# Block-sparse attention and a token/channel mixer: the queries of two more pairs of heads and the mask biases of two more pairs are turned by DMA, under a new order of the work

## Chip, cores and metric

The kernel runs on one core of one Trainium2 chip. The metric is the device time of one execution in microseconds; the time of a kernel is the median of its runs.

## The reference

Inputs are q, k and v, each [4, 8, 768, 64] (batch, head, position, width) in float32, and four weights. The core of the reference, with its shapes:

```python
k_rep = k.reshape(B, H, 12, 64, D).mean(axis=3)             # one mean key per block of 64
gate_scores = np.einsum('bhsd,bhnd->bhsn', q, k_rep)        # [B, H, 768, 12]
gate_scores = np.where(causal, gate_scores, -1e9)           # a query sees its own and earlier blocks
top_idx = np.argsort(gate_scores, axis=-1)[..., -3:]        # three best blocks, and the own block
...
mask = mask & (pos[:, None] >= pos[None, :])
scores = np.where(mask, scale * q @ k.T, -1e9)
attn_out = softmax(scores) @ v
...
x = attn_out.transpose(0, 2, 1, 3).reshape(4, 768, 512)
h = np.maximum(x.transpose(0, 2, 1) @ w_tok1, 0) @ w_tok2   # token mixing, 768 -> 256 -> 768
u = x + h.transpose(0, 2, 1)
h2 = np.maximum(u @ w_ch1, 0) @ w_ch2                       # channel mixing, 512 -> 1536 -> 512
out = u + h2
```

The three best blocks must be chosen as the reference chooses them, so the gate is computed from queries and key sums that are each held as the sum of two float16 numbers, a high part and a remainder.

## The kernel before

The 32 heads are worked on as 16 pairs, i = 0 to 15 (two heads of one batch side by side on 128 partitions). Four pairs make a batch, and when its attention is there, its mixer follows; pairs of the next batches run in between. A pair goes through these steps:

- **Loads** on the SP queue: `load_qk` (L379) brings ql (queries) and kl (keys) as two halves of 192 KB, `load_v` (L402) v.
- **Keys** are turned by six float32 transposes on TensorE (`transposes`, L436, tile tkl), evacuated from PSUM to kt (L482 ACT, L484 DVE), cast into KA, the operand of the scores (L806 on POOL, two casts per pair), and summed by block on DVE (`ksum`, L666, tile kst). POOL splits the sums in three small instructions (`split_sum`, L611 to L613; tiles ksums, kp).
- **Queries** are turned in one of two ways. For pairs below QTURN: six float32 transposes on TensorE (L436, tile tql), an evacuation to the high part qh (`evac_q`, L482 or L484) and one DVE instruction for the remainder qr, read from PSUM (`rest_q`, L520). From QTURN on: ACT scales and rounds ql to the high part (`split_hi`, L568, tile qn), DVE computes the remainder in SBUF (`split_rest`, L574), and two DMA transposes on the SP queue turn the two (`turn_q`, L579, to qh and qr). In both ways qh is copied into Q, the operand of the scores (`place_q`, two copies on POOL or ACT).
- **Gate**: ten matmuls qh, qr by kp (`gate_parts`, L644, tile gps), two additions on DVE (L656, L658), ten MAX8 (`top`, L675), a comparison (`below`, L685) and the mask bias bn (`bias`, L704), a float16 tile of 0 and -60000 per query and block.
- **Mask bias** turned in one of two ways. Below MTURN: five float16 transposes on TensorE (`mask`, L714, tile bps) and two copies into Q on DVE or ACT (`put_mask`, L804, L806). From MTURN on: one DMA transpose on the SP queue (`turn_m`, L693, tile mt) and two copies into Q on POOL or ACT (`place_m`).
- **Scores** (L736, tile sps), exponentials on ACT (L750, tile e), the diagonal's causal mask on DVE (L756) or POOL, attention times v (L772, tile aps), reciprocal and normalisation on DVE (L780, L791, tile x16).

The mixer of a batch: token products (L815, L827), u and its transpose uT by DMA (L421); the first channel product c = uT by wc1 (`ch1`, L896) with a relu on ACT (L798) or DVE (L800) to h2a and h2b; the second by seven block products (`prod`, L947) that need sums of h2 (s1, s3, s4) and four differences of the blocks of wc2: t3, t1, t2, t4 (`weight_sum`, L915, on DVE). The first three differences are taken once, before the first batch's second product; t3 is the first of them, and it reads all of the last half of wc2. The weights are loaded on POOL's queue: w for the tokens, wc1 in four loads (L1082), wc2 in four loads (L1084).

All this is written as a list of operations. `plan` (L225) puts them in the order of ORDER (L103) and sets from OTHER which operations run on their other engine, from LARGE which PSUM tiles take the larger kind, and from PLACES which copy of its buffer a tile takes. Each engine and each queue works in that order. A DMA transpose or a load is issued by SP when its turn comes, and SP waits at its head for the data that it reads or the buffer that it writes. So an operation's place in the list decides what waits behind it.

```python
QTURN = 10
MTURN = 9
...
            if t32 == "ql" and i >= QTURN:
...
            if i >= MTURN:
```

The first condition (L1117) chooses the way of the queries, the second (L1276) that of the mask bias.

## Time and profile before

| what | value |
|---|---|
| runs | 239.66, 238.57, 239.58 us |
| median | 239.58 us |
| profiled execution | span 237.6 us (the page gives the span alone) |
| instructions in the profile | 6633 |
| PE busy | 230.9 us, 97%, granted clock 0.9 or more of full speed in all 40 slices |
| DVE, ACT, POOL busy | 197.8, 158.5, 122.0 us |
| transfers | 35.60 MB, mean 150 GB/s |

The span runs from the profile's first instruction to its last. The median of the runs stands 1.98 us above it. Busy time is the time in which an engine had an instruction in work; PE is TensorE's matmuls, DVE VectorE, ACT ScalarE, POOL GpSimd, and SP the engine that issues most transfers. Idle time of an engine is put down to what ended it (its releaser).

### The profile page before, as it was taken

The numbers are of one execution on the slowest core, as the hardware profiler recorded it, in microseconds if no ns is written. First come the engines' busy times: TensorE is split into PE (matmuls) and PEld (weight loads), VectorE is DVE, ScalarE is ACT, GpSimd is POOL, SyncE is SP. The second block draws the span as 40 slices with busy tenths as digits, with TensorE's granted clock in tenths as the row PEclk, the third lists the DMA queues.
The fourth block names the chain that finished last, engine by engine and source line by source line (L and its number), as shares of the span: only waits on it lengthen the run. The fifth ranks groups of instructions, "written<-read, shape, count | busy, mean of one in ns | idle before, by whom it ended". The sixth has DMA issues, their size and how long they took to land.

```text
span 237.6 us, 6633 instructions
## 1 busy us (share of the span) xinstructions
PE 230.9 (97%) x2541; PEld 176.2 (74%) x2541; DVE 197.8 (83%) x604; ACT 158.5 (67%) x247; POOL 122.0 (51%) x214
## 2 busy tenths in 40 slices
PE   8899999999999999998999999999999999999994
PEld 6788889867777986784659885785768768666882
DVE  7999989999989999999799989995767678704861
ACT  6899998879879797869479675864778411064010
POOL 6899999258731364399530767354032132900560
PEclk9999999999999999999999999999999999999999
DMA  6999999999999698996936994973013015330033
GB/s 202 289 235 195 225 217 191 207 234 186 202 211 223 124 160 182 227 212 136 192 108 145 192 104 122 196 162 72 3 29 135 0 47 132 90 135 0 0 134 135
DMA packets 100208, 35.60 MB, mean 150 GB/s; under 512 B 90832, under 2 KB 96720, under 8 KB 100176
## 3 DMA queue, kind: packets, MB, share of 16 engines
q1 hardware_dynamic: 96400, 30.84, 58.7%
q0 software_dynamic: 3232, 3.93, 10.0%
q8 instruction: 20, 0.33, 0.6%
q10 hardware_dynamic: 544, 0.39, 0.5%
q14 instruction: 12, 0.10, 0.1%
HBM read 26.74 MB, written 6.29 MB: 139 GB/s over the span
## 4 chain that ended last, share of the span: by engine, by line
PE 84%; POOL 5%; DVE 4%; DMA 4%; ACT 1%; issue 1%; SPq 0%; ACTq 0%; DVEq 0%
PE c L896 24%; PE c L947 20%; PE sps L736 13%; PE aps L772 7%; PE ups L827 3%; PE tok L815 3%; DMA kl<-in_k_dram 2%; PE c L1003 2%; PE tkl L436 2%; POOL KA L806 2%; PE gps L644 1%; DMA mt<-bn 1%; POOL e L762 1%; PE tkl L449 1%; PE ups L860 1%; DVE qn L574 1%
## 5 line engine op out<-in xcount | busy, mean ns | idle before, releaser
L750 ACT ACTIVATE e<-sps 128x896 f16<-128x896 f32 (+2 forms) x96 | 84.7, 917 | 21.4 <-PE sps L736 20.8
L896 PE MATMUL c<-uT,wc 128*128 128x256 f16 (+1 forms) x384 | 69.4, 326 | 1.2 <-DVE h2a L800 1.2
L896 PEld LDWEIGHTS <-wc 128*128 128x128 f16 x384 | 36.3, 98 | 22.3 <-issue 1.7
L736 PE MATMUL sps<-Q,KA 128*128 128x128 f16 (+7 forms) x384 | 50.8, 259 | 0.3 <-ACT e L750 0.2
L969 POOL TENSOR_TENSOR vu<-v,u 128x256 f32<-128x256 f32 x33 | 24.9, 768 | 36.4 <-DVE v L962 35.0
L736 PEld LDWEIGHTS <-KA 128*128 128x128 f16 (+1 forms) x384 | 29.6, 97 | 13.9 <-issue 0.7
L806 POOL CAST KA<-kt 64x768 f16<-64x768 f32 x22 | 18.4, 836 | 19.9 <-ACT kt L482 18.1
L772 PE MATMUL aps<-V,e 128*128 128x65 f16 x672 | 25.6, 193 | 0.0
L772 PEld LDWEIGHTS <-e 128*128 128x128 f16 x672 | 24.2, 97 | 1.2
L798 ACT ACTIVATE h2a<-c 128x256 f16<-128x256 f32 (+1 forms) x27 | 13.0, 485 | 16.8 <-PE c L896 16.7
L947 PEld LDWEIGHTS <-s 128*128 128x128 f16 x198 | 18.9, 98 | 3.9
L800 DVE TENSOR_SCALAR h2b<-c 128x256 f16<-128x256 f32 (+1 forms) x24 | 13.2, 553 | 8.0 <-PE c L896 7.9
L791 DVE TENSOR_TENSOR x<-aps,rc 128x384 f16<-128x384 f32 x32 | 17.6, 551 | 0.4
L806 POOL COPY Q<-mt 12x320 f32<-12x320 f32 x10 | 4.9, 493 | 25.4 <-DMA mt<-bn 25.2
L947 PE MATMUL c<-t,s 128*128 128x256 f16 x132 | 17.7, 272 | 0.0
L756 DVE TENSOR_TENSOR e<-e,m 128x768 f16<-128x768 f16 x24 | 15.9, 668 | 1.9 <-ACT e L750 1.8
L800 DVE TENSOR_SCALAR h2a<-c 128x512 f16<-128x512 f32 (+1 forms) x21 | 11.5, 558 | 7.0 <-PE c L896 6.9
L798 ACT ACTIVATE h2b<-c 128x512 f16<-128x512 f32 (+1 forms) x24 | 11.5, 493 | 5.5 <-PE c L896 5.2
L947 PEld LDWEIGHTS <-h2a 128*128 128x128 f16 x132 | 12.5, 98 | 2.1 <-DVE h2a L932 0.2
L675 DVE MAX8 m<-gps 128x8 f32<-128x12 f32 x160 | 13.9, 160 | 0.2
L947 PEld LDWEIGHTS <-h2b 128*128 128x128 f16 x132 | 12.7, 98 | 1.8
L987 POOL TENSOR_TENSOR pc<-pc,pd 128x256 f32<-128x256 f32 x11 | 9.0, 817 | 8.6 <-ACT pc L804 6.5
(157 smaller groups left out, 456.7 us busy)
## 6 DMA issues: line engine op xcount, KB each, us to landing
v<-in_v_dram SPq DMA_DIRECT2D x16, 384.0 KB, 4.6
out_dram<-ob SPq DMA_DIRECT2D x23, 256.0 KB, 2.3
kl<-in_k_dram SPq DMA_DIRECT2D x28, 192.0 KB, 4.5
ql<-in_q_dram SPq DMA_DIRECT2D x26, 192.0 KB, 4.2
wc<-in_moe_w_ch_dram POOLq DMA_DIRECT2D x8, 384.0 KB, 8.4
kl<-in_k_dram SPq DMA_DIRECT2D x2, 384.0 KB, 5.7
ql<-in_q_dram SPq DMA_DIRECT2D x2, 384.0 KB, 7.1
w<-in_moe_w_tok_dram POOLq DMA_DIRECT2D x2, 384.0 KB, 7.9
```

The lines of the kernel that those rows point to most:

```text
L675: nc.vector.max(out=t[:, j, x, :], in_=T["gmx", i, m][:, j, x, :])
L736: nc.tensor.matmul(out=p[:, off + a:off + a + n], lhsT=KA[i % R][x][0:rows, 128 * kk:128 * kk + 128], rhs=QA[i % R][x][0:rows, q0 + a:q0 + ...
L750: nc.scalar.activation(out=e[:, 0:width], in_=T["sps", i, x, g][:, 0:width], func=AF.Exp, scale=scale)
L756: nc.vector.tensor_tensor(out=d, in0=d, in1=m0.broadcast_to([128, NJ, 128]), op=ALU.mult)
L772: nc.tensor.matmul(out=p[:, jq, :], lhsT=T["e", i, x, g][:, o:o + 128], rhs=V16[i % (R + 1)][:, x, kk, 0:65], start=(kk == 0), stop=(kk == ...
L791: nc.vector.tensor_tensor(out=T["x16", b][:, :, 64 * hh:64 * hh + 64], in0=T["aps", i, x][:, :, 0:64], in1=T["rc", i, x].broadcast_to([128 ...
L798: e.activation(out=out, in_=src, func=AF.Relu)
L800: e.tensor_scalar(out=out, in0=src, scalar1=0.0, scalar2=None, op0=ALU.max)
L806: e.tensor_copy(out=out, in_=src)
L896: nc.tensor.matmul(out=p, lhsT=wc1_16[:, cc, 128 * fc:128 * fc + 128], rhs=T["uT", b][:, a // 128:e // 128, cc, :], start=(cc == 0), stop= ...
L947: nc.tensor.matmul(out=T["c2" + key, b, j], lhsT=x[:, fc, :], rhs=y[:, fc, :], start=first and fc == 0, stop=fc == HF - 1, skip_group_chec ...
L969: nc.gpsimd.tensor_tensor(out=t, in0=T["v", b, j], in1=T["u", b][:, j + 3 * row, 256 * col:256 * col + 256], op=ALU.add)
```

## The change

Two numbers are changed: QTURN from 10 to 8 and MTURN from 9 to 7. So the queries of pairs 8 and 9 and the mask biases of pairs 7 and 8 take the way through the DMA transposes that the later pairs already took. No function is changed; each is three lines higher in the changed kernel, as ORDER is three lines shorter.

ORDER, OTHER, LARGE and PLACES are new throughout: every operation of the program may stand at another place, and the numbers of the operations are others, as some operations exist no more and others are new.

```diff
-QTURN = 10
+QTURN = 8
...
-MTURN = 9
+MTURN = 7
...
 ORDER = [
-    1471, 1479, 136, 137, 122, 123, 185, 184, 1459, 1468, 1483, 1465, 1476, 1464, 236, 1461, 1472, 1463, 1474, 1473,
...
+    288, 1475, 1463, 122, 2, 1472, 1478, 1477, 1461, 1482, 1465, 1486, 1464, 1466, 123, 137, 185, 3, 236, 0, 1474, 136,
...
```

What this makes of the engines' work: TensorE has 12 float32 transposes and 10 mask transposes fewer; SP issues 9 transposes of mask biases (7 before), 8 of qh and 8 of qr (6 and 6); DVE has 7 rows of work fewer and ACT 7 more, since some relus move from DVE to ACT; POOL has as many as before.

**SP, around the loads of the queries of pair 9** (a name's first number is the pair: kl_12 are the keys of pair 12; v32 is v). Before:

```order
L379 DMA kl_12_1436<-in_k_dram 128x6x64 x2
L379 DMA kl_9_1464<-in_k_dram 128x6x64 x2
L379 DMA ql_9_1562<-in_q_dram 128x6x64 x2
L379 DMA kl_10_1755<-in_k_dram 128x6x64 x2
L402 DMA v32_7_1811<-in_v_dram 128x12x64
L379 DMA ql_10_1838<-in_q_dram 128x6x64 x2
L402 DMA v32_8_1869<-in_v_dram 128x12x64
L379 DMA ql_11_1890<-in_q_dram 128x6x64 x2
```

After:

```order
L399 DMA v32_5_1504<-in_v_dram 128x12x64
L376 DMA kl_8_1518<-in_k_dram 128x6x64 x2
L576 DMA_TRANSPOSE qh_8_1527<-qn_8_1493 128x6x128
L576 DMA_TRANSPOSE qr_8_1600<-qn_8_1493 128x5x128
L399 DMA v32_6_1602<-in_v_dram 128x12x64
L690 DMA_TRANSPOSE mt_7_1673<-bn1_86 128x5x128
L376 DMA ql_9_1678<-in_q_dram 128x6x64 x2
L376 DMA kl_9_1842<-in_k_dram 128x6x64 x2
L376 DMA kl_10_1926<-in_k_dram 128x6x64 x2
L399 DMA v32_7_1931<-in_v_dram 128x12x64
```

Before, loads follow one another. Now the two transposes of pair 8's queries and the one of pair 7's mask bias (bn1) stand between the loads of keys 8 and queries 9, and the loads of keys 12, queries 10 and 11 stand later.

**POOL, around the split of pair 8's key sums** (KA and Q are operands of the scores, wc2 the weights of the second channel product; the first two of its four loads stand three rows ahead of the first piece). Before:

```order
L611 TENSOR_TENSOR ksums1_80<-kst_7_1458,heads_81 128x24
L612 CAST kp1_84<-ksums1_80 128x2x12
L613 TENSOR_TENSOR kp1_84<-ksums1_80,kp1_84 128x2x12
L1084 DMA wc2_90<-in_moe_w_ch2_dram 128x3x512
L806 COPY Q31_75<-qh_7_1352 64x384
L1084 DMA wc2_90<-in_moe_w_ch2_dram 128x3x512
L806 CAST V1_64<-v32_6_1376 128x12x64
L806 CAST KA_76<-kt_8_1637 64x768
L806 COPY Q30_74<-qh_7_1352 64x384
L611 TENSOR_TENSOR ksums0_79<-kst_8_1656,heads_81 128x24
L612 CAST kp0_83<-ksums0_79 128x2x12
L613 TENSOR_TENSOR kp0_83<-ksums0_79,kp0_83 128x2x12
```

After, where two earlier loads of wc2 stand ahead of the piece:

```order
L803 CAST V0_63<-v32_5_1504 128x12x64
L803 CAST KA_76<-kt_7_1323 64x768
L1081 DMA wc2_90<-in_moe_w_ch2_dram 128x3x512
L803 CAST KA_76<-kt_8_1630 64x768
L608 TENSOR_TENSOR ksums0_79<-kst_8_1676,heads_81 128x24
L609 CAST kp0_83<-ksums0_79 128x2x12
L610 TENSOR_TENSOR kp0_83<-ksums0_79,kp0_83 128x2x12
L803 COPY Q30_74<-qh_7_1362 64x384
L803 CAST KA_76<-kt_8_1630 64x768
L1081 DMA wc2_90<-in_moe_w_ch2_dram 128x3x512
L803 COPY Q31_75<-mt_7_1673 12x320
L803 COPY Q00_68<-qh_8_1527 64x384
```

Before, all four loads of wc2 stand ahead of pair 8's sums (ksums0 from kst_8). Now the third stands just ahead of them, and the fourth behind them, one copy of queries and one cast of keys. Pair 7's mask is copied by POOL from mt behind that load.

**DVE, from pair 8's gate to the first weight differences** (t3 and t1; gps is the gate, bn0 the mask bias of pair 8, e0 exponentials before the diagonal's mask). Before, where the first of the two copies of mask 7 stands two rows ahead of the piece, and pair 8's key sums and remainder three and two ahead of that copy:

```order
L806 COPY Q31_75<-bps_1709 12x640
L791 TENSOR_TENSOR x16_1_1444<-aps_1658,rc_1729 128x6x64
L756 TENSOR_TENSOR e0_6_1_1715<-e0_6_1_1715,m0_102 128x768
L800 TENSOR_SCALAR h2b_0_1335<-c1_1723 128x256
L656 TENSOR_TENSOR gm_8_1765<-gps_1736,gbias_100 128x120
L658 TENSOR_TENSOR gps_1736<-gps_1736,gm_8_1765 128x10x12
L675 MAX m8_8_1798<-gps_1736 128x8 x10
L685 TENSOR_TENSOR gps_1736<-gps_1736,m8_8_1798 128x10x12
L930 TENSOR_TENSOR s3_0_0_1825<-h2a_0_1330 128x768
L800 TENSOR_SCALAR h2a_0_1330<-c1_1760 128x256
L780 RECIPROCAL rc_1835<-aps_1776 128x6
L915 TENSOR_TENSOR t3_93<-wc2_90 128x1536
```

After, with pair 8's key sums eight rows ahead of the piece:

```order
L927 TENSOR_TENSOR s3_0_0_1768<-h2a_0_1325 128x768
L682 TENSOR_TENSOR gps_1716<-gps_1716,m8_8_1742 128x10x12
L701 SCALAR_TENSOR_TENSOR bn0_85<-gps_1716,own_101 128x10x12
L797 TENSOR_SCALAR h2b_0_1332<-c1_1730 128x512
L753 TENSOR_TENSOR e0_7_1_1773<-e0_7_1_1773,m0_102 128x768
L777 RECIPROCAL rc_1828<-aps_1775 128x6
L571 SCALAR_TENSOR_TENSOR qn_9_1797<-ql_9_1678,qn_9_1797 128x640
L753 TENSOR_TENSOR e0_6_1_1714<-e0_6_1_1714,m0_102 128x768
L788 TENSOR_TENSOR x16_1_1462<-aps_1775,rc_1828 128x6x64
L912 TENSOR_TENSOR t3_93<-wc2_90 128x1536
L753 TENSOR_TENSOR e0_7_0_1837<-e0_7_0_1837,m0_102 128x768
L912 TENSOR_TENSOR t1_91<-wc2_90 128x1536
```

Before, t3 stands behind the reciprocal that follows the gate's comparison. Now the mask bias, a relu, two diagonal masks, a normalisation and the remainder of pair 9's queries (qn_9) stand between the comparison and t3, and the copies of mask 7 are gone from DVE.

## Rows read from the trace of the kernel before

**Rows 1.** The page's part 1: busy us, share of the span, instructions
```profile
PE 230.9 (97%) x2541; PEld 176.2 (74%) x2541; DVE 197.8 (83%) x604; ACT 158.5 (67%) x247; POOL 122.0 (51%) x214
```

**Rows 2.** The page's part 4: the chain that ended last, by engine
```profile
PE 84%; POOL 5%; DVE 4%; DMA 4%; ACT 1%; issue 1%; SPq 0%; ACTq 0%; DVEq 0%
```

**Rows 3.** Two windows: us, PE, PEld, DVE, ACT, POOL busy, clock, DMA share, GB/s
```profile
48.00:60.00 12.00, 11.84 (x129) 8.21 (x128) 11.73 (x32) 9.82 (x18) 8.27 (x15) 1.00 1.02 204
60.00:72.00 12.00, 12.00 (x166) 9.23 (x164) 10.90 (x42) 9.52 (x15) 6.06 (x11) 1.00 1.19 207
```

**Rows 4.** The chain of waits, 79 to 84: start us, us, what
```profile
81.13 0.69 PE tql L436 x6
81.82 0.28 PE bps L714 x5
```

**Rows 5.** Groups by line and form: busy us, mean ns, idle before
```profile
L714 PE MATMUL bps<-id,bn 128*128 128x128 f16 x45 | 4.2, 219 | 0.2 <-DVE bn L704 0.2
L436 PE MATMUL tql<-id,ql 128*128 128x128 f32 x12 | 1.7, 277 | 0.0
```

**Rows 6.** Tiles qn and qr: ns min/median/max, first and last start us, forms
```profile
L568 ACT ACTIVATE qn<-ql x6: 827/839/846, 85.0 to 149.3; 128x768 f16<-128x768 f32 x6
L574 DVE SCALAR_TENSOR_TENSOR qn<-ql,qn x6: 810/816/2239, 89.9 to 150.8; 128x640 f16<-128x640 f32 x6
...
L520 DVE SCALAR_TENSOR_TENSOR qr<-tql,qh x2: 825/825/825, 66.5 to 82.8; 128x640 f16<-128x640 f32 x2
```

**Rows 7.** Timelines of DVE, POOL and PE, 108 to 114: start us, us, what
```profile
108.62 2.24 DVE L574 SCALAR_TENSOR_TENSOR qn<-ql,qn 128x640 f16<-128x640 f32 x1
...
108.90 0.50 POOL L806 COPY Q<-qh 64x384 f32<-64x384 f32 x1
...
112.45 1.89 PE L896 MATMUL c<-uT,wc 128*128 128x512 f16 x8 [1.07 <-DVE h2a L800]
```

**Rows 8.** Tile mt: instructions as in rows 6; landing us min/median/max
```profile
L806 POOL COPY Q<-mt x10: 441/446/717, 91.5 to 177.8; 12x320 f32<-12x320 f32 x10
L693 SPq DMA_TRANSPOSE mt<-bn x7: 1202/1211/1857, 88.1 to 173.3; - x7
...
DMA to landing us min/median/max: 2.6/2.8/4.2
```

**Rows 9.** Tile wc: landing of the weight loads, us
```profile
DMA to landing us min/median/max: 6.9/8.4/10.3
```

**Rows 10.** Timeline of POOL, 58 to 62: start us, us, what
```profile
58.04 0.50 POOL L806 COPY Q<-qh 64x384 f32<-64x384 f32 x1
...
60.20 0.80 POOL L1084 DMA_DIRECT2D wc<-in_moe_w_ch_dram  x1
...
61.51 0.78 POOL L1084 DMA_DIRECT2D wc<-in_moe_w_ch_dram  x1
```

**Rows 11.** Timeline of DVE, 65 to 74
```profile
65.01 0.95 DVE L666 TENSOR_REDUCE kst<-kt 128x12 f32<-128x768 f32 x1
...
69.24 0.54 DVE L791 TENSOR_TENSOR x<-aps,rc 128x384 f16<-128x384 f32 x1
69.70 0.54 DVE L756 TENSOR_TENSOR e<-e,m 128x768 f16<-128x768 f16 x1
...
73.13 0.92 DVE L915 TENSOR_TENSOR t<-wc 128x1536 f16<-128x1536 f16 x1
```

**Rows 12.** DMA issues, 49 to 52 and 57 to 59: KB each, median us to landing
```profile
ql<-in_q_dram SPq DMA_DIRECT2D x2, 192.0 KB, 4.4
kl<-in_k_dram SPq DMA_DIRECT2D x2, 192.0 KB, 4.2
...
wc<-in_moe_w_ch_dram POOLq DMA_DIRECT2D x2, 384.0 KB, 7.8
ql<-in_q_dram SPq DMA_DIRECT2D x2, 192.0 KB, 13.5
kl<-in_k_dram SPq DMA_DIRECT2D x1, 192.0 KB, 8.9
```

219 rows, old and new, of tables (LARGE, ORDER, OTHER, PLACES) are left out of this document.

## The prediction

> **What bounds the kernel now.** I read the busy line first: TensorE (PE) is busy for 230.9 of 237.6 us, VectorE (DVE) for 197.8, ScalarE (ACT) and GpSimd (POOL) for less [rows 1]. A busy share can hide waits, so the chain that ended last comes next: 84% of it is PE work, 4% DMA, 5% POOL, 4% DVE [rows 2]. So PE's own work sets the end, and a microsecond taken off PE is a microsecond won, unless another engine or a transfer then comes late. The stretch that the change works in is 48 to 72 us. There PE has next to no idle time at the full clock, DVE is busy for 11.73 and 10.90 of 12 us, and the DMA engines are full (1.02 and 1.19, overlapping packets counted twice) [rows 3]. DVE and the transfers are therefore next in line, and what is put on them there has little cover.
>
> The profiled execution has a span of 237.6 us; the page gives no time for what lies around it. The median of the three runs shown, 239.58, is 1.98 above the span. I add every term to the median, which supposes that these 1.98 us stay. A difference under 0.5%, 1.2 us, is what a measurement of this kernel can't tell from no change.
>
> **What leaves PE.** Two pairs lose six float32 transposes each, and two pairs lose five mask transposes each. In the chain, six float32 transposes take 0.69 us and five mask transposes 0.28 us [rows 4]. That is 2 x 0.69 + 2 x 0.28 = 1.9 us, and all of it lies on PE, with no wait before or behind. **Term 1: -1.9 us.** The rows of single transposes read 277 and 219 ns [rows 5]; these are latencies that overlap, since six of 277 would be 1.66 us and not 0.69. The Trainium skill ("TensorE: Matmul & The Clock Gate", Part 4: PE-mode transpose) gives about 275 ns per transpose in one kernel's context, which is the latency of the rows; as a price it would make the gain larger, and that is a rival below.
>
> **What other engines get.** Pairs 8 and 9 exchange one evacuation on ACT for one scaled split on ACT, and one remainder on DVE (0.825 us from PSUM) for one remainder on DVE (median 0.816, worst 2.239) [rows 6]. These cost the same, unless the remainder collides. One did: at 108.62 us it took 2.24 us while POOL worked without a break; the diagonal mask and the relu behind it on DVE were late by as much, and PE stood for 1.07 us at 112.45 [rows 6, 7]. It is the largest stall of PE after the start. In the new order another instruction may meet POOL there, or none. One of six remainders collided, and there will be eight, so one such stall somewhere is likely; but its cost hangs on what stands behind it. The ends are 0 and 1.1 us of gain, and I take the middle. **Term 2: -0.6 us** (-1.1 to 0).
>
> The mask copies of pairs 7 and 8 move from DVE and ACT to POOL and ACT, which wait for the transposes instead. POOL had room there, so I cost them at nothing. If POOL gave no cover, two copies of 0.45 us would be late by 0.9 us at pair 7; that end is in the range.
>
> **What the queues get.** SP issues six transposes more: the two of pair 8 and the mask of pair 7 now stand between the loads of k 8 and q 9 (first pair of order rows). Such a transpose lands 2.6 to 4.2 us after its issue, median 2.8 [rows 8]. Pair 7's mask bias is two DVE instructions ahead of pair 8's k sums, so the mask lands some 3 us after it and POOL copies it 0.5 us later; PE has over six other groups of matmuls up to pair 7's first scores. I cost this wait at nothing, and up to 1.4 us if it lands after 4.2.
>
> The Trainium skill ("VectorE: DVE Perf Modes", The three transpose paths and Rules for kernel authors) speaks against the change: it advises TensorE for a 128x128 transpose where PSUM will do, and gives 1309 ns for one by DMA against 390 on TensorE. By it five tiles would take 6.5 us, an estimate; the rows have 2.8 for the five, so here the measurement decides. By the page the mask of pair 7 would be about 1 us late, and the result within 0.5%.
>
> The weights are the edit that I think decides. All four wc2 loads stood before the k sums of pair 8 on POOL; now the last one stands behind them and behind two copies (second pair of order rows). Before, the last load was issued at 61.51 and DVE began the first weight difference, which needs all four, at 73.13: 11.6 us for a landing of 6.9 to 10.3 us, median 8.4 [rows 9, 10, 11]. Now count from the end of pair 8's k sums on DVE:
> - POOL does the copy of q, the cast of k, three small instructions for the sums, and then issues the load. The same five took from 58.04 to 60.20 us: 2.2 us [rows 10]. With a landing of 7.8 us (the two issued first, with little else of their queue in flight [rows 12]) the weights are there after 10.0 us; with 6.9 or 10.3, after 9.1 or 12.5.
> - DVE took from 65.96 (65.01 + 0.95) to 73.13 for what stood between, 7.2 us [rows 11]. Now one diagonal mask and one normalisation stand there more, and two mask copies less (third pair of order rows): about 7.5 us.
> - So DVE stands for 2.5 us (1.6 to 5.0). Behind it wait the diagonal mask of pair 7, the second difference and PE's first product that reads it. That product comes 9.3 us of matmuls after pair 8's gate (in the new order, at the chain's pace), and DVE needs 7.6 us plus the latency of 0.3 from the same gate to the end of the second difference. So 1.4 us are covered. **Term 3: +1.1 us** (0.2 to 3.6).
>
> **Sum:** -1.9 - 0.6 + 1.1 = -1.4 us, so 239.6 - 1.4 = **238.2 us**. Its own range goes from -1.9 - 1.1 + 0.2 = -2.8 (236.8) to -1.9 - 0 + 2.0 (239.7).
>
> **Rivals.**
> 1. *No change that can be told.* The weights land as late as the median and the collision comes back. Then term 3 is 2.2 - 1.4 - 7.5 + 8.4 = 1.7, up to 3.0 with the mask's wait (1.3 of the 1.4), and term 2 is 0: -1.9 + 1.7 to 3.0, about 239.9. For it: the stretch is full of transfers already [rows 3]. Against it: loads of k 12, k 14, q 10 and q 11 that stood here are issued later now.
> 2. *Slower: the load of q 9 lands late.* It stands directly behind the mask's transpose on SP, which waits for pair 7's bias. That bias leaves DVE 1.4 us before the k sums end; 1.2 us of issue for the transpose and two issues put the second half of q 9 at 1.0 us after the k sums. ACT splits it (0.84) and DVE's remainder of pair 9, three instructions ahead of the weight difference, waits for that. Up to a landing of 6.4 us it hides behind the weights (10.0 - 1.0 - 0.84 - 1.75 for the three). Loads of half a pair landed in 4.2 and 4.4 us with no weights in flight, but in 8.9 and 13.5 us when issued beside them [rows 12]. With 10.5 us the weight difference starts at 14.1 us instead of 7.5; less the 1.4 covered, PE loses 5.2, and ACT's exponentials queue behind the same split. So -1.9 - 0.6 + 5.2 = +2.7, **242.3 us**. It decides from a landing of 9.0 us on (+1.2 us). Against it: those slow ones had four weight loads and four halves of k around them; here the queue holds one load of v and one transpose just ahead, and one or two weight loads beside.
> 3. *Each transpose costs its latency.* 12 x 0.277 + 10 x 0.219 = 5.5 us off PE: 239.6 - 5.5 - 0.6 + 1.1 = 234.6. The chain speaks against it: six in 0.69 us [rows 4]. It is what the skill's figure in Part 4 would give.
>
> **How the numbers follow.** The forecast gets 0.55: 0.42 for below 238.4 and 0.13 for above. Rival 1 gets 0.20, rival 2 0.20, rival 3 0.03, and 0.02 is left for a new order that also removes the small stalls of the start. Faster by over 0.5%: 0.42 + 0.03 + 0.02 = 0.47. Within 0.5%: 0.13 + 0.20 = 0.33. Slower by over 0.5%: 0.20. The range leaves out rival 3 and the upper part of rival 2, some 0.16 together: 236.4 to 241.8 us, with 0.4 below the forecast's own end for the remainder.
>
> **What would show it.** Right: PE's busy time falls by about 1.9 us and its largest stall lies near 72 to 78 us, before a product that reads a weight difference, with DVE idle just ahead of the first difference on wc2; transposes of pairs 8 and 9 and of masks 7 and 8 landing in 2.6 to 5 us; no PE idle before the scores of pair 7. Term 3 is wrong if DVE has no idle time ahead of the first difference. Rival 2 shows as ACT idle on q before a split near 70 to 76 us, with that load landing after 9 us or more. The whole argument is wrong if PE's busy time doesn't fall, or if the new stalls lie outside 60 to 80 us, where I have priced nothing but the old one at 112 us.

## The result, and the profile after

| | median of the runs | profiled span |
|---|---|---|
| before | 239.57 us (238.57 to 239.66) | 237.6 us |
| after | 241.70 us (241.50 to 242.57) | 240.0 us |

The ratio of after to before is 1.0102, with a 95% interval of 1.0064 to 1.0140: the change makes the kernel slower by 2.4 us (1.5 to 3.4). All results below are such ratios against runs of the kernel before on the same chip, with the disturbed runs left out, so a difference of medians can differ from what the ratio gives. In microseconds a ratio is taken times 239.5.

Busy times of the profile after (they answer to [rows 1]) and, below them, its chain of waits by engine ([rows 2]):

```profile
PE 230.2 (96%) x2519; PEld 173.8 (72%) x2519; DVE 197.0 (82%) x597; ACT 162.6 (68%) x254; POOL 122.1 (51%) x214
```

The chain's shares:

```profile
PE 69%; POOL 9%; DVE 7%; DMA 5%; ACT 4%; issue 3%; SPq 2%; POOLq 0%; ACTq 0%; DVEq 0%
```

The 22 transposes are gone from PE (2541 matmuls before, 2519 now). Its busy time fell by only 0.7 us, though, and its idle time rose from 237.6 - 230.9 = 6.7 to 240.0 - 230.2 = 9.8 us. PE's share of the chain fell from 84% to 69%; what took its place is the other engines, DMA and SP's queue.

Windows of the profile after, columns as in [rows 3]:

```profile
60.00:72.00 12.00, 11.95 (x157) 8.74 (x156) 10.22 (x43) 11.86 (x20) 7.34 (x13) 1.00 1.17 179
72.00:84.00 12.00, 11.29 (x121) 9.13 (x120) 11.01 (x20) 11.11 (x20) 1.86 (x5) 1.00 1.05 176
84.00:96.00 12.00, 10.19 (x116) 7.20 (x113) 9.97 (x31) 8.71 (x14) 5.81 (x9) 1.00 1.14 207
108.00:120.00 12.00, 11.79 (x90) 7.11 (x87) 10.42 (x21) 10.06 (x16) 9.37 (x16) 1.00 1.07 194
```

From 72 to 96 us PE idles for 0.71 + 1.81 = 2.52 us. Before, it idled for nothing there. The DMA engines stay full up to 96 us and beyond, and DVE and ACT, which looked like the next bounds, have idle time as well: they wait too. In 108 to 120 us PE idles for 0.21 us, where the old stall of 1.07 us was.

Where the new idle time begins is seen in the chain of waits of the profile after, 68 to 91 us (start us, us, what):

```profile
68.59 3.64 DMA ql<-in_q_dram
...
83.74 4.96 DMA ql<-in_q_dram
...
88.80 0.85 ACT qn L565
...
89.68 0.83 DVE qn L571
```

and in the timelines of the profile after (start us, us, instruction, the wait before it and who ended it), first of ACT:

```profile
73.05 0.84 ACT L565 ACTIVATE qn<-ql 128x768 f16<-128x768 f32 x1 [0.81 <-DVE h2b L797]
...
88.80 0.84 ACT L565 ACTIVATE qn<-ql 128x768 f16<-128x768 f32 x1 [1.52 <-DMA ql<-in_q_dram]
```

of PE:

```profile
74.85 0.59 PE L733 MATMUL sps<-Q,KA 76*128 76x512 f16 x3 [0.71 <-ACT e L747]
...
90.39 0.59 PE L733 MATMUL sps<-Q,KA 128*128 128x512 f16 x3 [1.12 <-ACT e L747]
...
94.02 0.83 PE L944 MATMUL c<-t,h2a 128*128 128x256 f16 x6 [0.70 <-DVE h2a L929]
```

and of DVE:

```profile
76.01 0.96 DVE L912 TENSOR_TENSOR t<-wc 128x1536 f16<-128x1536 f16 x1 [0.33 <-issue]
```

The same thing happens twice. The load of queries 9, and then that of queries 10, is the last thing to come. ACT stands before the split of these queries; its exponentials queue behind the split, and PE stands before scores whose PSUM tile ACT has not read. At 73.05 the wait is put down to a DVE relu, which ended at 72.72 and which the split doesn't read; the chain goes back to the load. Its second half was issued at 68.55 and is listed as landed after 4.3 us, at 72.9, just before the split (its last transfer ended at 72.23 in the chain). At 88.80 DVE's remainder waits for the split in turn, and that makes the third stall of 0.70 us. The first weight difference, which the prediction feared for, waits for 0.33 us and stops nobody.

### The profile page after: what moved, and what is told of

Read it like the earlier page. It is cut to its first block, busy times and chain, and to the rows that moved or that the text cites. A ratio compares the mean times of both kernels' runs of the same rounds, so it can differ in the third digit from the quotient of the medians.

```text
span 240.0 us, 6634 instructions
## 1 busy us (share of the span) xinstructions
PE 230.2 (96%) x2519; PEld 173.8 (72%) x2519; DVE 197.0 (82%) x597; ACT 162.6 (68%) x254; POOL 122.1 (51%) x214
## 4 chain that ended last, share of the span: by engine, by line
PE 69%; POOL 9%; DVE 7%; DMA 5%; ACT 4%; issue 3%; SPq 2%; POOLq 0%; ACTq 0%; DVEq 0%
PE c L893 24%; PE c L944 15%; PE sps L733 9%; PE aps L769 6%; DMA ql<-in_q_dram 4%; POOL KA L803 3%; PE c L1000 2%; PE ups L824 2%; PE tok L812 2%; ACT e L747 2%; POOL Q L803 2%; PE warm L1019 2%; DMA out_dram<-ob 1%; POOL e L759 1%; PE ups L857 1%
## 5 line engine op out<-in xcount | busy, mean ns | idle before, releaser
L747 ACT ACTIVATE e<-sps 128x768 f16<-128x768 f32 (+2 forms) x96 | 85.5, 924 | 18.1 <-PE sps L733 12.9
L893 PE MATMUL c<-uT,wc 128*128 128x512 f16 (+1 forms) x384 | 70.0, 326 | 0.2 <-DVE rc L777 0.2
L733 PEld LDWEIGHTS <-KA 76*128 76x128 f16 (+1 forms) x384 | 29.9, 97 | 16.3 <-issue 3.2
L795 ACT ACTIVATE h2a<-c 128x512 f16<-128x512 f32 (+1 forms) x30 | 15.0, 500 | 12.4 <-PE c L893 12.1
L803 POOL CAST KA<-kt 64x768 f16<-64x768 f32 x22 | 19.4, 882 | 2.9 <-ACT kt L479 2.3
L797 DVE TENSOR_SCALAR h2b<-c 128x512 f16<-128x512 f32 (+1 forms) x22 | 12.4, 566 | 7.0 <-PE c L893 7.0
L795 ACT ACTIVATE h2b<-c 128x256 f16<-128x256 f32 (+1 forms) x26 | 12.4, 485 | 7.6 <-PE c L893 7.6
L753 DVE TENSOR_TENSOR e<-e,m 128x768 f16<-128x768 f16 x24 | 15.3, 643 | 1.1 <-ACT e L747 1.1
L803 POOL COPY Q<-mt 12x320 f32<-12x320 f32 x13 | 6.6, 507 | 15.9 <-DMA mt<-bn 15.5
L797 DVE TENSOR_SCALAR h2a<-c 128x256 f16<-128x256 f32 (+1 forms) x18 | 9.6, 539 | 4.8 <-PE c L893 4.6
```

What stands on the lines that cost most here:

```text
L733: nc.tensor.matmul(out=p[:, off + a:off + a + n], lhsT=KA[i % R][x][0:rows, 128 * kk:128 * kk + 128], rhs=QA[i % R][x][0:rows, q0 + a:q0 + ...
L747: nc.scalar.activation(out=e[:, 0:width], in_=T["sps", i, x, g][:, 0:width], func=AF.Exp, scale=scale)
L753: nc.vector.tensor_tensor(out=d, in0=d, in1=m0.broadcast_to([128, NJ, 128]), op=ALU.mult)
L795: e.activation(out=out, in_=src, func=AF.Relu)
L797: e.tensor_scalar(out=out, in0=src, scalar1=0.0, scalar2=None, op0=ALU.max)
L803: e.tensor_copy(out=out, in_=src)
```

## The experiments

The theories: **A**, two loads stand too late in SP's order; **B**, the stretch from 57 to 96 us has no room for six more transposes, either in SP's issue time (**B1**) or in the transfers themselves (**B2**); **C**, the last load of wc2 is in the way; **D**, the cost is in other places that the new order moved. All results in one table, with PE's idle time in windows of the profile (12 us less PE's busy time):

| run | ratio to before (95%) | us | idle 60-72 | 72-84 | 84-96 | 96-108 | 108-120 |
|---|---|---|---|---|---|---|---|
| before | 1 | 0 | 0.00 | 0.00 | 0.00 | 0.00 | 1.07 |
| after | 1.0102 (1.0064 to 1.0140) | +2.4 | 0.05 | 0.71 | 1.81 | 0.27 | 0.21 |
| e1_q10 | 1.0096 (1.0061 to 1.0131) | +2.3 | 0.04 | 0.79 | 1.23 | 0.48 | 0.08 |
| e2_q9 | 1.0108 (1.0059 to 1.0157) | +2.6 | 0.95 | 1.35 | 0.34 | 0.04 | 0.21 |
| e3_q9q10 | 1.0131 (1.0087 to 1.0176) | +3.1 | 0.72 | 1.38 | 0.35 | 0.04 | 0.01 |
| e4_wc2 | 1.0161 (1.0112 to 1.0211) | +3.9 | 1.39 | 2.13 | 0.26 | 0.05 | 0.00 |
| f1_vpool | 1.0093 (1.0063 to 1.0124) | +2.2 | 0.77 | 0.00 | 0.91 | 1.17 | 0.10 |
| f2_extra | 1.0234 (1.0141 to 1.0327) | +5.6 | 0.00 | 3.08 | 0.00 | 1.94 | 1.06 |
| f3_pemask | 1.0045 (1.0019 to 1.0070) | +1.1 | 0.13 | 0.14 | 0.37 | 0.20 | 0.28 |
| f5_gap | 1.0398 (1.0345 to 1.0451) | +9.5 | 3.07 | 4.06 | 0.03 | 0.28 | 0.24 |
| g1_none | 1.0001 (0.9983 to 1.0018) | 0.0 | 0.04 | 0.00 | 0.58 | 0.00 | 0.74 |
| g2_traffic | 1.0101 (1.0068 to 1.0135) | +2.4 | 0.81 | 2.55 | 0.26 | 0.04 | 0.05 |
| g3_masks | 1.0013 (1.0000 to 1.0026) | +0.3 | 0.05 | 0.21 | 0.21 | 0.28 | 0.00 |
| g4_late | 1.0012 (0.9990 to 1.0034) | +0.3 | 0.00 | 0.00 | 0.00 | 0.00 | 1.11 |
| h1_after_free | 0.9980 (0.9959 to 1.0001) | -0.5 | 0.05 | 0.10 | 0.28 | 0.00 | 0.34 |
| h2_before_free | 1.0014 (0.9997 to 1.0031) | +0.3 | 0.00 | 0.00 | 0.00 | 0.00 | 1.05 |
| h4_shift | 0.9953 (0.9935 to 0.9970) | -1.1 | 0.00 | 0.00 | 0.00 | 0.00 | 0.00 |

### Loads moved ahead in SP's order, and the weights on POOL's

The moves are made in `plan`, on operation numbers (624 loads queries 10, 580 queries 9, 891 the last part of wc2, each set behind the second number):

```diff
 def plan(ops, rings):
+    for n, at in ((624, 499), (580, 540),):
+        ORDER.remove(n), ORDER.insert(ORDER.index(at) + 1, n)
```

These two pairs are e3_q9q10. The run e1_q10 has the first alone, e2_q9 the second alone, and e4_wc2 has (891, 893).

> The changed kernel (241.7 us) with the load of queries 10 moved ahead on SP, from behind the three transposes of pairs 9 and 8 and the load of v 8 to directly behind the load of v 7: issued at about 76.7 us instead of 83, while its buffer is free from 74.7. Theory A (late loads: SP issues in order, so each transpose put ahead of a load makes it late; ACT's split of the queries waits for it, and exponentials and a DVE remainder queue behind the split): the split of pair 10 no longer waits (1.52 us in the changed kernel), the PE stalls of 1.12 us at 90.4 and of 0.70 at 94 go, and the time falls by 1.2 to 1.9 us, to 239.8 to 240.5. Theory B (the transfers themselves are full between 60 and 96 us, so what is moved ahead makes another transfer as late): the stall moves to another load or transpose, the time stays within 0.5 us of 241.7. Theory C (the last load of wc2, issued at 68.7 us, is what slows SP's loads): no change here.

> The changed kernel with the load of queries 9 moved ahead on SP, from behind the load of v 6 and the transpose of mask 7 to ahead of both: issued at about 64.2 us instead of 68. Theory A: the split of pair 9 on ACT no longer waits (0.81 us), PE's stall of 0.71 us at 74.8 goes, and the time falls by 0.5 to 0.9 us, to 240.8 to 241.2. Theory B: within 0.5 us of 241.7. A variant of B: mask 7 and v 6 come 1.2 us later, and PE waits for the scores of pair 7 instead; then 241.7 or more. Theory C: no change.

> Both moves together. Theory A: the effects add, 1.8 to 2.8 us less than the changed kernel, 238.9 to 239.9, so level with the kernel before (239.6). Theory B: within 0.5 us of 241.7. Theory C: no change.

> The changed kernel with the last load of wc2 moved ahead on POOL, from behind the key sums of pair 8 to directly behind the third load of wc2: issued at about 62.4 us instead of 68.7. Theory C: the loads of keys 9 and 10 (four issues in 6.6 us on SP) go faster, what stands behind them on SP is issued 1 to 3 us earlier, and the time falls by 1 us or more. The prediction's term 3 (DVE waits for the weights at the first difference) would give at most the 0.33 us that DVE stands there in the changed kernel, so under 0.4 us. Theory A: no change (within 0.5 us), or a loss if the weights beside them make the loads of v 6 and queries 9 land later.

None of them is faster: +2.3, +2.6, +3.1 and +3.9 us against +2.4 for the change. What moved is the stall. The wait of ACT for queries 10 did go in e1_q10, but mask 8, now behind that load, came late: POOL waited 1.58 us for it instead of 0.80, and PE stood 0.66 us, up to 85.5 us, for POOL's copy of it into the operand of the scores. In e2_q9, e3_q9q10 and e4_wc2 the mask of pair 7 is the late one. From the timeline of POOL of e2_q9, and from its PE's waits (tile, line, releaser: us in total, times, longest):

```profile
72.85 0.44 POOL L803 COPY Q<-mt 12x320 f32<-12x320 f32 x1 [3.36 <-DMA mt<-bn]
```

```profile
PE sps L733 <- POOL Q L803: 2.3, 1, 2.3
```

POOL waits 3.36 us for the mask (0.83 in the kernel after), and PE 2.3 us for POOL. So A falls: none of the places tried is right for all of them. C falls as well: with the weights earlier the time did not fall. What stood beside them became later (ACT waited 3.52 us for v 6), and the time rose by a further 1.4 us, though the intervals of the two runs overlap.

### The same bytes from another queue

```diff
-            nc.sync.dma_start(out=t.rearrange("p g j d -> p (g j) d"),
+            (nc.gpsimd if i in (6, 7, 8) else nc.sync).dma_start(out=t.rearrange("p g j d -> p (g j) d"),
```

> The changed kernel with the loads of v 6, 7 and 8 issued by POOL instead of SP (POOL is idle from 72 to 81 us). The bytes are the same, SP has three issues fewer between 64 and 83 us. Theory A has fallen with the first four runs: a load moved ahead on SP made a mask's transpose late instead. Theory B1 (SP's own issue time is the limit between 57 and 96 us): the transposes of pair 9 and mask 8 and the load of queries 10 are issued 1 to 2 us earlier, PE's idle time in 84 to 96 us falls from 1.81 to under 0.8, the time by 0.8 to 1.5 us. Theory B2 (the transfers themselves are the limit: the DMA engines are full and SP only waits to hand over): PE's idle time and the time stay within 0.5 us.

+2.2 us instead of +2.4, with PE's idle time in 84 to 96 us at 0.91 and 1.17 us more behind it. SP did come forward, as B1 foresaw: queries 10 were issued at 79.82 us instead of 82.97. Other transfers became late in their place: the remainder's transpose of pair 8 landed after 6.7 us instead of 5.1, and PE stood for it for 0.77 us. Three issues less on SP gave nothing that can be told, which speaks against B1 and for B2. The transposes' own issues stayed on SP, so B1 is not excluded for these by this run alone. The Trainium skill ("Trainium Kernel Development and Optimization", Key Constraints) says that DMAs from the SP, ACT and POOL queues share the same 16 engines and that a second queue saves issue time only; this run agrees.

### Three loads moved into the gap on SP

SP stands from 58.98 to 62.92 us at the second transpose of pair 8, which waits for DVE. Three loads were put ahead of it, with (580, 539), (617, 580), (451, 617) in `plan`:

> The changed kernel with three loads moved ahead on SP into the gap that SP spends waiting at the second transpose of pair 8 (59 to 62.9 us: it waits for the remainder from DVE with the queue behind it): queries 9, keys 10 and v 6 now stand between the two transposes of pair 8. No load is added. Theory B1 or B2: 3.0 us of issue are done in time that was idle, everything behind (mask 7, keys 9, v 7, the transposes of pair 9, mask 8, queries 10) is issued 1.5 to 3 us earlier, PE's idle time in 72 to 96 us falls from 2.5 to under 1, and the time by 1.2 to 2.2 us, to 239.6 to 240.6. If it is only how many transfers are in flight that counts, they land later instead, and the gain is under 0.5 us. Theory D: no change.

A miss, and the plainest one: +9.5 us. The gap in SP's issues was no gap in the transfers. The remainder's transpose, now behind three loads, was issued at 66.28 us instead of 62.92, as the issues of these loads took until then, and landed after 9.7 us instead of 5.1. PE's gate of pair 8 waited for it. From PE's timeline and from the windows of f5_gap:

```profile
76.06 0.22 PE L641 MATMUL gps<-kp,qr 128*128 128x48 f16 x1 [7.08 <-DMA qr<-qn]
```

```profile
72.00:78.00 6.00, 1.94 (x13) 0.94 (x14) 1.23 (x11) 0.83 (x1) 1.21 (x3) 0.61 1.34 185
78.00:84.00 6.00, 6.00 (x63) 4.63 (x62) 4.36 (x13) 4.28 (x8) 0.12 (x1) 0.82 0.24 51
```

The stall cost more than its 7.08 us: the third number from the end of a window's row is the granted clock, 0.61 and 0.82 of full speed in the two windows from 72 to 84 us, against 1.00 in the rest. PE's busy time rose with it, to 232.2 us against 230.2 in the kernel after.

### Six transposes more in the kernel before, early and late

In f2_extra the kernel before, its order untouched, issues six transposes of a piece of wc1 to places that nobody reads:

```diff
+            for tag in {("kl", 9): ["ob_0"], ("ql", 9): ["ob_1"], ("kl", 10): ["more"], ("ql", 11): ["kh_0", "ob_2"], ("kl", 14): ["more"]}.get((t32, i), []):
+                to = sp.tile([128, DM] if tag[0] == "o" else [128, S // 2], FP, tag=tag, bufs=1, name=f"x{t32}{i}{tag}").bitcast(F16)
+                turn(to[:, 0:S].rearrange("p (j t) -> p j t", t=128), wc1_16[:, 0, 0:S])
```

In g4_late the same six stand behind the transpose of the last mask:

```diff
+            for n in range(6 if i == 15 else 0):
+                to = sp.tile([128, S], FP, tag=f"{'qk'[n // 3]}l_{n % 3}", bufs=1, name=f"x{n}").bitcast(F16)
+                turn(to[:, 0:S].rearrange("p (j t) -> p j t", t=128), wc1_16[:, 0, 0:S])
```

> The kernel before, with its order as it is, and six more DMA transposes on SP between the loads of keys 9 and keys 11, each of a 128x768 piece of wc1 to a place that nobody reads (one behind keys 9, queries 9, keys 10, two behind queries 11, one behind keys 14). Nothing waits for their results; they cost queue and transfer time alone, as many as the change adds. Theory B (either form): the loads and transposes behind them come late, PE gets idle time of 1.5 to 4 us between 72 and 108 us (0.0 before), and the time rises by as much, to 240.8 to 243.3. Theory D (the cost of the change is in the other places that the new order moves, such as the small stalls at 12 to 36 and at 140 us, or in DVE and ACT): within 0.5 us of the kernel before.

> The kernel before with the same six extra transposes as in the run that had them between 57 and 91 us (+8 us there), now issued one behind another at 175 us, where the DMA engines are busy for a tenth of the time and SP waits for outputs. Theory B2: nothing is in their way and no load stands behind them, so the time stays within 0.5 us of the kernel before (239.5). If a transpose costs by itself, wherever it stands (SP's issue, a shared buffer), 1 us or more.

Early they cost 5.6 us (3.4 to 7.8), more than foreseen; late, nothing that can be told (-0.2 to +0.8). The 5.6 rest on two runs, of 243.34 and 246.78 us, and the profile is of the second; the 8 us named in the text above are a difference of medians. DMA issues of f2_extra, 57 to 92 us, and of g4_late, 174 to 184 us (tile, queue, operation, issues, KB where given, median us from issue to landing):

```profile
wc<-in_moe_w_ch_dram POOLq DMA_DIRECT2D x4, 384.0 KB, 13.2
...
xkl9ob<-wc SPq DMA_TRANSPOSE x1, 14.1
xql9ob<-wc SPq DMA_TRANSPOSE x1, 12.2
xkl10more<-wc SPq DMA_TRANSPOSE x1, 3.9
xql11kh<-wc SPq DMA_TRANSPOSE x1, 4.7
xql11ob<-wc SPq DMA_TRANSPOSE x1, 2.8
xkl14more<-wc SPq DMA_TRANSPOSE x1, 4.5
```

```profile
x<-wc SPq DMA_TRANSPOSE x6, 2.8
```

Transposes that land in 2.8 us where the engines are idle take 12.2 and 14.1 us beside the four loads of wc2, and 2.8 to 4.7 behind these. The four loads of wc2 stand on POOL's queue and were issued at the same times as before, within 0.2 us, yet they land after 13.2 us in the median. In the kernel before the same row reads:

```profile
wc<-in_moe_w_ch_dram POOLq DMA_DIRECT2D x4, 384.0 KB, 8.6
```

So here it is neither SP's issue time nor its order that makes the weights late. DVE stands for 3.41 us before the first weight difference, and PE behind it (timeline of f2_extra):

```profile
78.08 1.07 PE L899 MATMUL c<-uT,wc 128*128 128x512 f16 x4 [3.08 <-DVE bn L707]
```

From 78 to 84 us the granted clock has a mean of 0.72, and PE's busy time is 233.1 us instead of 230.9, so part of the 5.6 us is the clock and not the wait.

Part 3 of the pages gives the time that the packets of SP's queue took, as a share of 16 engines' span (packets, MB, share). Before, f2_extra, g4_late, and then g1_none (of the next section) and the kernel after:

```profile
q1 hardware_dynamic: 96400, 30.84, 58.7%
```

```profile
q1 hardware_dynamic: 101200, 32.02, 64.3%
```

```profile
q1 hardware_dynamic: 101200, 32.02, 60.9%
```

```profile
q1 hardware_dynamic: 96400, 30.84, 62.1%
```

```profile
q1 hardware_dynamic: 100688, 31.89, 63.0%
```

Times the spans (237.6, 245.1, 238.6, 238.5 and 240.0 us) that is 139.5, 157.6, 145.3, 148.1 and 151.2 us. With the six transposes the sum is 5.8 us higher late and 18.1 us higher early. These are not prices of a transpose, though: overlapping packets are counted twice, and the order alone moves the sum as much. g1_none has the same packets as the kernel before and 8.6 us more, and from there to the change the six add 3.1 us.

### The added transposes taken out, wholly and in part

In g1_none the six added transposes are left out and their readers read a piece of wc1; g3_masks leaves out only the four of the queries; g2_traffic issues all six and only lets the readers read elsewhere. The edit of g1_none:

```diff
     def turn_q(i, c):
         def f():
+            if i in (8, 9):
+                T[("qh", "qr")[c], i] = wc1_16[:, c, 0:S - 128 * c]
+                return
...
             T["mt", i] = t
+            if i in (7, 8):
+                T["mt", i] = wc1_16[:, 2, 0:S - 128].rearrange("p (j t) -> p j t", t=128)
+                return
```

> The changed kernel without the six transposes that it adds (qh and qr of pairs 8 and 9, masks of pairs 7 and 8): their readers read a piece of wc1 instead, so those results are not the reference's; every other instruction and the order stay. Theory B2 (a transpose holds the transfer engines while it moves little, in a stretch that was full): PE's idle time in 72 to 96 us falls from 2.5 to under 0.5, and the time by 2 to 3 us, to 238.7 to 239.7. This is what the change would give if transposes cost nothing. If the small stalls at 12 to 36 and 140 us were the cost (theory D), it stays above 241.

> The changed kernel with the same six transposes issued, but nobody waits for them: their readers read the piece of wc1, as in the run without them, so the results are not the reference's. It keeps the transposes' traffic and their place in SP's queue, and takes away only the waits for their own landing. Theory B2: what costs is the traffic that makes the loads of queries 9 and 10 late, so the time stays at 241 to 242 and PE's idle time in 72 to 96 us above 1.5. Rival (B3: it is the transposes' own landing that PE, POOL and ACT wait for): the time falls to that of the run without them, 238.7 to 239.7.

> The changed kernel without the four transposes of the queries of pairs 8 and 9 (their readers read a piece of wc1, so those results are not the reference's), with the two of masks 7 and 8 in place. The masks alone were worth 1.2 us with the 0.56 of TensorE's work against it, so some 1.5 to 1.8 us. Theory B2, costs that add by the number of transposes: the four give back at least half of what all six give, 1 to 2 us, so 239.8 to 240.8. If the masks carry it (they stand between loads and wait for DVE at the head of the queue): under 0.7 us.

Without the six the kernel stands level with before, so D falls for the 2.4 us. With the six issued, and no engine waiting for what they bring, it stands at +2.4 us, as the change does. So it isn't the wait for the transposes' own landing that costs, but what they do to the loads beside and behind them. From SP's timelines of g1_none and then of g2_traffic, the loads of queries 9 and what SP stands at before them:

```profile
57.59 2.25 SPq L376 DMA_DIRECT2D ql<-in_q_dram  x2
```

```profile
62.80 2.23 SPq L576 DMA_TRANSPOSE qr<-qn  x1
...
68.34 1.17 SPq L376 DMA_DIRECT2D ql<-in_q_dram  x2
```

The load that comes late is above all issued late: at 57.59 us without the six, at 67.97 in the kernel after and 68.34 in g2_traffic, while its halves landed after 6.9 us in the median in g1_none and 3.8 in the kernel after. Before it SP stands until 62.80 us at the second transpose of pair 8, whose source DVE makes, and this wait is in g2_traffic too. So SP's standing there is a rival that g2_traffic doesn't exclude. f2_extra, whose transposes read a weight that is long there, shows that the cost arises without such a wait, but in the order of the kernel before; how the 2.4 us divide between SP's waits, its issue time and slower transfers stays open.

Windows of g1_none, then of g2_traffic, 72 to 84 us:

```profile
72.00:84.00 12.00, 12.00 (x147) 10.00 (x145) 11.67 (x22) 11.90 (x21) 3.41 (x6) 1.00 0.44 92
```

```profile
72.00:84.00 12.00, 9.45 (x111) 7.55 (x111) 8.28 (x15) 10.06 (x18) 0.61 (x2) 1.00 1.13 217
```

The DMA share is 0.44 without them and 1.13 with them, in the same order of work: without them the loads that SP can issue are done by about 77 us, and the DMA engines rest (a share of 0.02 from 77.5 to 82.7 us). In g2_traffic the stall comes from other victims than in the kernel after, the load of v 6 (ACT waits for it 1.61 us) and again queries 9.

The mask biases by themselves, undone in f3_pemask:

```diff
-MTURN = 7
+MTURN = 9
...
 def plan(ops, rings):
+    for n, at in ((506, 950), (507, 944), (508, 507), (971, 965), (550, 522), (551, 511), (552, 551)):
+        ORDER.remove(n), ORDER.insert(ORDER.index(at) + 1, n)
```

(506 and 550 are the masks of pairs 7 and 8, given a PSUM bank in PLACES; 507, 508, 551 and 552 their copies, put on DVE in OTHER; 971 is a channel product that makes room.)

> One part of the change undone: the mask biases of pairs 7 and 8 turned on TensorE again (MTURN = 9) within the new order, their copies on DVE; the queries of pairs 8 and 9 stay on the DMA transposes. TensorE gets 2 x 0.28 = 0.56 us more work, DVE four copies of 0.45 us. Theory B: SP has two transposes fewer (65.3 and 80.2 us), which gives back 2 to 4 us of its time, so the loads of queries 9 and 10 come earlier and PE's idle time in 72 to 96 us falls from 2.5 to under 1.2; with the 0.56 the time falls by 0.5 to 1.2 us. Theory D: the stalls stay, the time rises by 0.5 us. If DVE becomes late by the four copies, PE waits for relus at 70 or 79 us, and the time rises too.

+1.1 us instead of +2.4: taking out the two mask transposes alone is worth 1.3 us, although TensorE takes back 0.56 us of work. Taking out the four of the queries alone is worth 2.4 - 0.3 = 2.1 us. Together these would be more than the 2.4 that all six are worth. The excess of 1.0 us is about as large as the noise of the three runs, so it is a sign and no proof that there is no price per transpose, and that the others cost little once the first are gone.

### What is left of the gain

g1_none leaves a question: TensorE has 1.9 us less work in it than in the kernel before, and takes the same time.

> The changed kernel without any transpose of queries or masks by DMA (pairs 8 to 15 and 7 to 15): their readers read a piece of wc1, so those results are not the reference's. The run without the six added ones stood level with the kernel before (239.45), though TensorE has 1.9 us less work; this asks where those 1.9 us are. Theory F1 (the later transposes, which both kernels have, still cost in the new order): 1.5 us or more below 239.45. Theory F2 (the rest is waits of TensorE for DVE, ACT and POOL that the new order has at 7 to 35, 91, 110 and 138 us, and no transfer): within 0.6 us of 239.45.

> The kernel before without any transpose of queries or masks by DMA (pairs 10 to 15 and 9 to 15), in the same way. Theory F1: little to gain there, since PE's idle time in 72 to 108 us is 0.0: within 0.6 us of 239.5, and the changed kernel without any is 1 us or more faster than this one. Theory F2: both are level within 0.6 us, so the 1.9 us of TensorE's work are lost to waits for other engines in the new order.

Without any transpose of queries or masks by DMA, the kernel after stands at -0.5 us (-1.0 to 0.0), the kernel before at +0.3 (-0.1 to +0.7). So the later transposes, which both have, don't carry the rest. The difference of 0.8 us (0.2 to 1.5) lies between what F1 and F2 foresaw, and it is all that the new order turns into time even with free transfers. It holds the end of the old stall too: PE's idle time in 108 to 120 us is 1.05 us in h2_before_free and 0.34 in h1_after_free. Waits of PE in g1_none, where the rest of its new idle time is (us in total, times, longest):

```profile
PE c L899 <- DVE ob L986: 0.7, 1, 0.7
PE c L950 <- DVE h2a L935: 0.5, 1, 0.5
PE kps L551 <- DVE ob L984: 0.5, 1, 0.5
```

The kernel before doesn't have these waits for DVE. In the first 36 us PE idles for 0.6 us more (3.0 against 2.4), and what was added there are waits for ACT and POOL. What makes these engines late wasn't tried. Nor is it settled why PE's busy time is only 0.8 us lower in g1_none and g3_masks, and 0.9 between the two kernels without any DMA transpose (230.4 and 231.3); the profile models the ends of matmuls, so short gaps can count as busy.

### The old stall by itself

Term 2 of the prediction was tried in the kernel before, by moving the remainder of pair 12 (712) behind the two relus, with its transpose (714):

```diff
 def plan(ops, rings):
+    for n, at in ((712, 1083), (714, 712),):
+        ORDER.remove(n), ORDER.insert(ORDER.index(at) + 1, n)
```

> The kernel before with one DVE instruction moved: the remainder of the queries of pair 12, which took 2.24 us beside POOL at 108.6 us and made PE stand for 1.07 us, now stands behind the two relus that PE waited for (and its transpose on SP behind it). If that stall is worth its length, as term 2 of the prediction has it: 0.5 to 1.1 us less than the kernel before, 238.4 to 239.0. If the next instruction on DVE or the next stall takes its place: within 0.4 us.

-1.1 us (-0.7 to -1.6): faster than both kernels. The timelines of DVE and PE of h4_shift answer to [rows 7]:

```profile
109.03 1.54 DVE L756 TENSOR_TENSOR e<-e,m 128x768 f16<-128x768 f16 x1 [0.41 <-ACT e L750]
110.49 1.28 DVE L800 TENSOR_SCALAR h2a<-c 128x512 f16<-128x512 f32 x2
111.69 0.81 DVE L574 SCALAR_TENSOR_TENSOR qn<-ql,qn 128x640 f16<-128x640 f32 x1
```

```profile
110.27 2.84 PE L896 MATMUL c<-uT,wc 128*128 128x512 f16 x12
```

The relus end 1.2 us earlier, and the twelve matmuls run through without a gap. The remainder now takes 0.81 us instead of 2.24; the diagonal mask beside POOL took 1.54 instead.

## Why the prediction was wrong, point by point

- **What bounds the kernel.** PE with DVE and the transfers next in line, and little cover in 48 to 72 us: right, and the warning was in [rows 3]. The step from it, that a microsecond taken off PE is a microsecond won, failed.
- **Term 1, -1.9 us.** The 22 matmuls are gone. But with every DMA transpose of queries and masks free in both kernels, the difference is 0.8 us, and the end of the old stall (term 2) is in it. So term 1 brought little: PE's busy time fell by 0.7 to 0.9 us, and other waits, for DVE, ACT and POOL, came with the new order. The rival that took a transpose for its latency (234.6 us) is out.
- **Term 2, -0.6 us.** The stall at 112 us is gone in the kernel after (0.21 us idle in its window instead of 1.07), and h4_shift prices it at 1.1 us: right, and nearer to its upper end of 1.1 than to the middle.
- **Term 3, +1.1 us.** The last load of wc2 was issued at 68.67 us, 2.1 us after the end of the key sums, and landed after 7.3 us, much as worked out. The wait that I foresaw was 0.33 us instead of 2.5, since the work ahead of it on DVE was itself late (done 9.1 us after the key sums instead of 7.5), and PE lost nothing by it. The sum's upper end, 239.7, takes 2.0 us for this term, whose own range goes to 3.6; that was a slip.
- **The step that failed** is "I cost this wait at nothing", for the six transposes on SP. I priced each by its own landing (2.8 us, hidden by PE's other work) and looked for who waits for it. What it does to the loads beside and behind it had no term in the sum (rival 2 counted one issue of 1.2 us), and the three transposes ahead of queries 10 were not followed at all. [rows 3] showed DMA shares of 1.02 and 1.19, and [rows 8] were taken from 88 us on; the mask of pair 7 landed after 5.0 us, and the first transpose of pair 8 after 7.6. g1_none against the change prices that term at 2.4 us, and g2_traffic shows that it is there when nobody waits for the transposes. How much of it is SP's standing and how much slower transfers stays open.
- **Rival 2, 242.3 us,** is near the measured 241.7 and has the right chain: the load of queries 9 late, ACT's split and DVE's remainder waiting, exponentials queued behind. Its condition, a landing of 9.0 us or more, was not met: the load landed after 4.3 us. It was issued later, its second half 2.0 us after the key sums instead of 1.0, since the mask's transpose ahead of it held SP for 2.68 us instead of 1.2, and PE lost 0.7 us there and not 5.2; the rest came from the same thing at queries 10. That it could be cured by the load's place was my reading after the result, and e1 to e3 and f5_gap refute it for the places tried.
- **The advice of the Trainium skill** ("VectorE: DVE Perf Modes", Rules for kernel authors) to turn 128x128 on TensorE where PSUM will do, which I set aside because five tiles landed in 2.8 us, holds in this stretch: f3_pemask, which follows it for two masks, is some 1.3 us faster than the change (0.3 to 2.5).
- **What would show it.** I wrote that the argument is wrong if PE's busy time doesn't fall or the stalls lie outside 60 to 80 us. It fell by 0.7 us instead of 1.9, and 1.81 of the 2.57 us of idle time between 60 and 96 lies behind 84.

## What to carry to other kernels

Before work is moved from a busy engine to DMA, look at the DMA share of the stretch where it lands: at a share near 1 a transfer was paid for here by the loads beside and behind it, even where nobody waited for it, and changing places in the queue only chose who was late. What a transfer costs where the engines rest is no price for a full stretch: the same six transposes cost 0.3 us, not to be told from nothing, at 175 us, and 5.6 us between 57 and 91. Look as well at what a transpose makes the queue wait for, since the loads behind it wait along. And a stall whose releaser is one instruction on another engine is worth a try by itself: moving that instruction won 1.1 us, where the whole change was forecast to win 1.4 and lost 2.4.

## What the runs showed of the hardware

- The same DMA transpose of 128x768 float16 elements landed after 2.8 us where the DMA engines were idle (g4_late), and after 12.2 and 14.1 us beside loads of weights (f2_extra). These loads, on another queue, then landed after 13.2 us in the median instead of 8.6.
- A long stall of PE costs more than its length. Behind 7.08 us of waiting in f5_gap the granted clock had a mean of 0.61 in 72 to 78 us and 0.82 in 78 to 84, so part of that time was run at the lower of the two levels, 1.2 instead of 2.4 GHz. Behind 3.08 us of waiting in f2_extra the mean was 0.72 in 78 to 84 us.
- A DVE instruction that ran beside POOL's copies and cast near 109 us took nearly three times as long: the remainder 2.24 instead of 0.81 us in the kernel before, the diagonal mask 1.54 instead of 0.54 us when it stood in that place. That POOL is the cause is read from the place alone; no run took POOL's work away.
